# The last 128-row output tile of a fused attention and MoE kernel, computed as two 256-column halves in two PSUM banks

## The chip, the cores and the metric

One core of a Trainium2 chip runs the kernel. The metric is the device time of one execution in microseconds (us). Before the change the median of 4 runs is 301.82 us (301.5 to 302.29). One further quantity is used throughout: the profiled execution, whose own time is 301.5 us and whose span, from its first to its last recorded instruction, is 299.7 us. About 0.2% (0.6 us) is what a measurement of this kernel can tell from no change.

## The reference

The reference computes a linear attention (softmax of q over the head dimension, softmax of k over the sequence, k-transposed times v, then q times that) and feeds the result as rows into a two-layer network with an ELU between. Only the last step is touched by the change, the second matrix product:

```python
h = x @ w_in                      # x: 4608 x 512, w_in: 512 x 2048
g = np.where(h > 0.0, h, np.exp(np.minimum(h, 0.0)) - 1.0)
return (g @ w_out)                # w_out: 2048 x 512, result 4608 x 512, float32
```

## The kernel before

The 4608 rows are worked in 9 blocks of 512. For each block, eight groups `g` compute 256 rows of the transposed hidden layer (line 543, 16 matmuls of 512 columns into a two-bank PSUM tile), ScalarE (ACT) takes the exponential (line 559), VectorE (DVE) finishes the ELU and writes the group into the tile `GT` in SBUF (lines 576 and 578). The second product follows one block behind: a 128-row output tile `ts` of a block `jb` is a sum over 16 slices `jj` of `GT`, so 16 matmuls, each with its own 128x128 weights (a slice of `GT`) and 512 moving columns (a slice of `W2`), all in fp32r, into one PSUM bank (`out_mm`, line 582, matmul on line 588). Every matmul instruction is a weight load (shown as PEld) and a matmul (shown as PE).

`out_store` (line 595) then has ACT copy the bank to one of three SBUF tiles `OSB` (line 605) and sends two stores of 64 rows of 2,048 bytes (128 KB each) to DRAM (line 615). All stores go through SP's queue, but the second one of the very last tile is issued from ACT's (line 614), so that the last two stores are issued at once.

After the last block's groups, nothing is left but output tiles: the last half of the block before's last tile, and then the four tiles `ts` = 0 to 3 of the last block (lines 797 to 802), alternating between PSUM banks 4 and 5. The first of them is split in 14 and 2 matmuls, as the last group of `GT` arrives late.

What runs on which engine in which order is not left to a scheduler: `ORDER` holds a table of operation numbers for each engine, written out by hand. Numbers are given in the order in which `add` is called. `Sched.order` walks the tables with an estimate of every duration only to merge the engines into one program; within an engine the table's order holds. `Sched.emit` (line 178) puts a semaphore wait before an operation for each dependency on another engine or a DMA. At the end SP waits for all store semaphores whose names begin with "o" (lines 223 to 225), in the order in which they were made; there are 15.

Of the kernel before, what the change touches and what calls it, by code (L numbers as in the profile page):

```python
# [3 lines left out]
AF = mybir.ActivationFunctionType  # L4
# [7 lines left out]
B, H, S, D = 8, 8, 576, 64  # L12
DFF = 2048
BLK = 512
NBLK = B * S // BLK
RING = 3 * BLK
NU = 2 * B
CH = 9
# [3 lines left out]
ISSUE = {"sp": 550, "act": 550, "gp": 740}  # L22
# [7 lines left out]
        "518 461 496 469 501 526 509 564 514 572 522 538 585 527 540 568 577 573 598 581 586 590 594 "  # L30
        "603 611 549 607 636 599 556 657 640 612 662 644 649 653 645 670 622 666 624 683 688 658 679 "
        "632 675 671 634 696 709 684 692 701 714 697 705 722 727 735 718 710 740 731 748 723 744 761 "
        "736 766 757 753 749 770 787 762 774 779 775 783 788 792 793 797 801 805 "),
    "act": (
        "3 22 33 23 24 31 29 34 35 48 44 55 73 76 77 79 83 84 87 94 95 97 104 91 92 116 117 119 98 "
        "108 120 127 135 133 163 160 179 147 166 154 169 205 176 230 231 188 234 180 240 241 191 246 "
# [3 lines left out]
        "493 467 484 531 489 453 460 463 506 519 462 497 470 502 542 510 515 565 537 523 539 554 551 "  # L40
        "528 569 578 574 541 552 616 582 591 587 595 548 555 550 608 637 600 626 557 604 641 613 650 "
        "654 621 646 623 663 667 689 631 625 659 680 633 676 672 685 693 715 702 698 635 706 719 728 "
        "711 732 741 724 745 737 767 758 750 771 754 763 776 780 784 789 794 798 802 806 808 "),
    "dve": (
        "2 4 5 0 6 7 25 26 37 27 38 39 40 41 42 36 46 49 51 52 53 56 74 75 78 80 81 85 88 89 96 100 "
        "105 106 101 102 122 118 110 111 112 123 124 141 142 143 148 155 182 183 184 177 178 232 206 "
# [14 lines left out]
        "229 228 323 315 288 295 316 289 324 298 341 359 308 360 377 307 340 393 370 371 406 394 420 "  # L61
        "380 407 419 447 433 390 465 482 432 458 448 389 494 481 495 459 468 478 507 520 535 477 567 "
        "508 521 536 553 566 546 580 547 579 620 605 638 606 593 592 630 651 652 639 677 665 690 664 "
        "678 703 716 717 691 730 704 729 756 768 769 742 755 743 782 791 781 790 800 795 799 796 803 "
        "804 807 "),
}


# [159 lines left out]
def t_act(n, psum):  # L228
    return n / 1.2 + (70 if psum else 99)


def t_dve(n, fast=1):
    return n / 0.96 / fast + 74


def t_f32r(n):
    return (n + 32) / 2.4


class Gen:  # L240
# [338 lines left out]
                gt, esb[:, :], P[:, :], ALU.max), key,  # L579
                R=[f"E{i}"], W=gw, X=banks)  # L580

    def out_mm(self, jb, ts, bk, jj0, jj1, key):
        S = self.S
        GT, dst = self.GT[jb % 2], self.bank(bk)

        def mm(e):
            for jj in range(jj0, jj1):
                last = e.matmul(dst, GT[:, jj, ts * 128:(ts + 1) * 128], self.W2[:, jj, :],  # L588
                                start=(jj == 0), stop=(jj == 15))
            return last  # L590
        S.add("pe", (jj1 - jj0) * t_f32r(512), mm, key, side=2,
              R=[f"G{jb % 2}_{g}" for g in range(jj0 // 2, (jj1 + 1) // 2)] +
                [f"W2_{s}" for s in range(jj0 // 4, (jj1 + 3) // 4)], X=[f"b{bk}"])

    def out_store(self, jb, ts, bk, key, eng="act"):
        S = self.S
        if jb == 0:
            i, osb = f"x{ts}", self.OSB0[ts]
        else:
            i = self.oslot % len(self.OSB)  # L600
            self.oslot += 1
            osb = self.OSB[i]
        src = self.bank(bk)
        if eng == "act":
            S.add("act", t_act(512, True), lambda e: e.activation(osb[:, :], src, AF.Copy), key,  # L605
                  W=[f"O{i}0", f"O{i}1"], X=[f"b{bk}"])
        else:
            S.add("dve", t_dve(512), lambda e: e.tensor_copy(osb[:, :], src), key,
                  W=[f"O{i}0", f"O{i}1"], X=[f"b{bk}"])
        rows = self.out.rearrange("(b p c) f -> b c p f", p=64, c=CH)  # L610
        for x in range(2):
            gi = 8 * jb + 2 * ts + x
            b, c = gi // CH, gi % CH
            q = "act" if x and gi == 8 * NBLK - 1 else "sp"
            S.add(q, ISSUE[q], lambda e, b=b, c=c, x=x: e.dma_start(
                rows[b, c], osb[x * 64:(x + 1) * 64, :]), key, R=[f"O{i}{x}"],
                dma=f"o{i}{x}{q}", nbytes=64 * 2048)
            S.ops[-1].packet, S.ops[-1].margin = 2048, 300

    def program(self):  # L620
        S = self.S
# [123 lines left out]
        key = 0  # L745
# [48 lines left out]
        assert not work  # L794
        self.out_mm(*w, key)
        self.out_store(w[0], w[1], w[2], key + 1)
        for ts in range(4):
            bk = 4 + ts % 2
            for jj0, jj1 in ((0, 14), (14, 16)) if ts == 0 else ((0, 16),):
                self.out_mm(NBLK - 1, ts, bk, jj0, jj1, key)  # L800
            self.out_store(NBLK - 1, ts, bk, key)
            key += 1


# [33 lines left out]
```

The softmax here doesn't subtract the row's maximum and nothing guards it: scores larger than these inputs give would overflow.

## Time and profile before

| What | Value |
|---|---|
| median of 4 runs | 301.82 us |
| profiled execution, its time | 301.5 us |
| profiled execution, its span | 299.7 us |
| what lies around the span (time less span) | 1.8 us |
| PE (TensorE matmul) busy | 287.0 us, 96% of the span |
| PEld (weight load) busy | 235.4 us, 79% |
| DVE busy | 189.5 us, 63% |
| ACT busy | 182.3 us, 61% |
| granted TensorE clock, mean | 0.998 |
| one 128x512 copy of a PSUM bank by ACT (line 605) | 597 ns |
| start of the last tile's first matmul | 292.23 us |
| start of the last tile's copy by ACT | 296.06 us |
| issue of the last two stores | 296.68 us |

An engine's share of the span says how busy it was; with PE at 96% the kernel is one long row of matmuls. A matmul's own duration in the profile (389 ns for 512 columns) is longer than the distance between the starts of two of them (227 ns), since they are pipelined: for the cost of a matmul the starts are to be read. "Time to landing" of a store runs from its issue until its semaphore is complete. Times within the execution are counted from the span's start.

### The profile page before, as it was taken

To read this page: it belongs to the slowest core of one execution; us is meant where nothing else is said; L and a number is where in the kernel's file an instruction comes from. 1 tells how busy PE (TensorE), PEld (TensorE's weight loads), DVE (VectorE), ACT (ScalarE), POOL (GpSimd) and SP (SyncE) were. 2 spreads that over 40 slices of the span, in tenths; PEclk is the share of its full clock that TensorE was granted. 3 is DMA by queue.
4 is the path that set the end of the run, shared out by engine and by line. 5 is a ranking of instruction groups with operands and counts; after the bars stand their busy time and mean duration, and the time that the engine had idled before them with its cause. 6 is when DMAs were issued, how large, how long until landed. Compare 5 with 4: busy or idle time off the path is not lost.

```text
span 299.7 us, 4412 instructions
## 1 busy us (share of the span) xinstructions
PE 287.0 (96%) x1849; PEld 235.4 (79%) x1849; DVE 189.5 (63%) x244; ACT 182.3 (61%) x211; POOL 21.7 (7%) x33
## 2 busy tenths in 40 slices
PE   1699999999999999999999999999999999999995
PEld 1578877677888888888888888888888888888883
DVE  3948934985898685894568855588437256655400
ACT  5758848998977967867755767534562423432411
POOL 0960234100000000000000000000000000000000
PEclk9999999999999999999999999999999999999999
DMA  7999998995497895289436236041311302004223
GB/s 263 388 399 391 388 391 257 235 328 198 118 277 229 125 363 172 76 258 276 163 116 167 87 90 159 2 104 40 78 44 44 72 0 53 0 0 107 56 60 94
DMA packets 35283, 49.96 MB, mean 167 GB/s; under 512 B 16320, under 2 KB 16320, under 8 KB 35264
## 3 DMA queue, kind: packets, MB, share of 16 engines
q1 hardware_dynamic: 29680, 34.09, 41.1%
q0 software_dynamic: 5504, 15.47, 16.1%
q8 instruction: 14, 0.23, 0.3%
q10 hardware_dynamic: 80, 0.13, 0.1%
q14 instruction: 5, 0.04, 0.0%
HBM read 36.70 MB, written 9.44 MB: 154 GB/s over the span
## 4 chain that ended last, share of the span: by engine, by line
PE 94%; DVE 2%; ACT 2%; DMA 1%; issue 0%
PE PS L588 44%; PE PS L543 43%; PE PS L487 3%; PE PS L456 2%; DMA QR<-in_q_dram 1%; PE PS L403 1%; DVE ZQ L372 1%; ACT ESB L559 1%; DVE QS L380 0%; DVE GT L572 0%; ACT QR L352 0%; PE PS L653 0%; ACT ESB L570 0%; ACT OSB L605 0%; DVE RZQ L376 0%
## 5 line engine op out<-in xcount | busy, mean ns | idle before, releaser
L588 PE MATMUL PS<-W,GT 128*128 128x512 f32 x576 | 141.2, 392 | 0.4 <-DVE GT L578 0.4
L543 PE MATMUL PS<-XT,W 128*128 128x512 f32 x576 | 140.4, 391 | 0.1
L543 PEld LDWEIGHTS PS<-XT,W 128*128 128x128 f32 x576 | 107.2, 188 | 23.0 <-DVE GT L572 0.5
L588 PEld LDWEIGHTS PS<-W,GT 128*128 128x128 f32 x576 | 106.8, 188 | 22.6 <-DVE GT L578 0.8
L559 ACT ACTIVATE ESB<-PS 128x1024 f32<-128x1024 f32 x72 | 73.7, 1027 | 64.9 <-PE PS L543 64.7
L576 DVE TENSOR_SCALAR ESB<-ESB 128x1024 f32<-128x1024 f32 x64 | 44.1, 691 | 66.6 <-ACT ESB L559 65.9
L578 DVE TENSOR_TENSOR GT<-ESB,PS 128x1024 fp32r<-128x1024 f32 x64 | 77.7, 1217 | 1.8
L605 ACT ACTIVATE OSB<-PS 128x512 f32<-128x512 f32 x32 | 18.8, 597 | 32.2 <-PE PS L588 32.0
L372 DVE TENSOR_REDUCE ZQ<-QR 128x18 f32<-128x1152 f32 x16 | 21.5, 1343 | 7.2 <-ACT QR L352 7.2
L509 ACT ACTIVATE XT<-PS 128x512 fp32r<-128x512 f32 (+6 forms) x32 | 19.5, 608 | 8.6 <-PE PS L487 8.1
L380 DVE TENSOR_TENSOR QS<-QR,RZQ 128x1152 f16<-128x1152 f32 x16 | 21.6, 1353 | 0.3
L352 ACT ACTIVATE QR<-QR 128x1152 f32<-128x1152 f32 x16 | 18.6, 1165 | 2.8 <-DMA QR<-in_q_dram 2.8
L356 ACT ACTIVATE KR<-KR 128x1152 bf16<-128x1152 f32 x16 | 18.5, 1160 | 1.7 <-DMA KR<-in_k_dram 1.7
L487 PE MATMUL PS<-qsT,MBLK 128*128 128x320 f32 (+5 forms) x64 | 14.4, 312 | 0.0
L431 ACT ACTIVATE qsT<-QT 128x1152 fp32r<-128x1152 f16 x12 | 14.0, 1165 | 0.3 <-DMA QT<-QS 0.3
L487 PEld LDWEIGHTS PS<-qsT,MBLK 128*128 128x128 f32 x64 | 11.9, 194 | 2.7 <-DVE MBLK L469 0.5
L365 ACT ACTIVATE VB<-VR 128x1152 bf16<-128x1152 f32 (+1 forms) x12 | 13.5, 1125 | 0.6 <-DMA VR<-in_v_dram 0.6
L572 DVE SCALAR_TENSOR_TENSOR GT<-PS,ESB 128x1024 fp32r<-128x1024 f32 x8 | 9.8, 1221 | 4.5 <-ACT ESB L570 4.4
L403 PE MATMUL PS<-ID,QS 128*128 128x128 f16 x36 | 3.7, 266 | 6.7 <-DVE QS L380 6.7
L469 DVE TENSOR_TENSOR MBLK<-PS,RZK 64x128 fp32r<-64x128 f32 x32 | 9.2, 288 | 0.9
L403 PEld LDWEIGHTS PS<-ID,QS 128*128 128x128 f16 x36 | 2.9, 122 | 7.3 <-DVE QS L380 7.0
L570 ACT ACTIVATE ESB<-ESB 128x1024 f32<-128x1024 f32 x8 | 8.5, 1060 | 0.2
(28 smaller groups left out, 60.0 us busy)
## 6 DMA issues: line engine op xcount, KB each, us to landing
out_dram<-OSB SPq DMA_DIRECT2D x63, 128.0 KB, 2.4
QR<-in_q_dram SPq DMA_DIRECT2D x12, 576.0 KB, 5.0
KR<-in_k_dram SPq DMA_DIRECT2D x12, 576.0 KB, 5.6
VR<-in_v_dram SPq DMA_DIRECT2D x12, 576.0 KB, 5.4
W<-in_moe_w_out_dram POOLq DMA_DIRECT2D x4, 1024.0 KB, 18.9
QR<-in_q_dram POOLq DMA_DIRECT2D x4, 576.0 KB, 11.4
KR<-in_k_dram POOLq DMA_DIRECT2D x4, 576.0 KB, 11.5
VR<-in_v_dram POOLq DMA_DIRECT2D x4, 576.0 KB, 8.1
```

The lines of the kernel that those rows point to most:

```text
L352: S.add("act", t_act(1152, False), lambda e: e.activation(flat(q), flat(q), AF.Exp), key - 3, X=[f"qR{i}"], follow=self.table)
L356: S.add("act", t_act(1152, False), lambda e: e.activation(ek[:, :, :, :].rearrange("p h c d -> p (h c d)"), flat(k), AF.Exp), key - 2, X=[ ...
L372: S.add("dve", t_dve(1152), lambda e: e.tensor_reduce(self.ZQ[i][:, :, :].rearrange("p h c -> p (h c)"), q[:, :, :, :].rearrange("p h c d ...
L380: S.add("dve", t_dve(1152), lambda e: e.tensor_tensor(qso, q[:, :, :, :], rz, ALU.mult), key - 3, R=[f"qR{i}", f"RZQ{i}"], W=[f"QS{self.al ...
L487: last = e.matmul(P[:, y:y + n_], M[:, f, :], T[:, c0:c1, f * 64:f * 64 + 64], start=True, stop=True)
L509: S.add("act", t_act((h1 - h0) * n_, True), lambda e, dst=dst, src=src: e.activation(dst, src, AF.Copy), key, W=W, X=X)
L543: last = e.matmul(P[:, t * 512:(t + 1) * 512], self.W1[:, kc, tt * 128:(tt + 1) * 128], self.XT[:, kc, rc:rc + BLK], start=(kc == 0), stop ...
L559: S.add("act", t_act(1024, True), lambda e: e.activation(esb[:, :], P[:, :], AF.Exp), key, W=[f"E{i}"], X=banks)
L576: S.add("dve", t_dve(1024, 2), lambda e: e.tensor_scalar(esb[:, :], esb[:, :], 1.0, -1.0, ALU.min, ALU.add), key, X=[f"E{i}"])
L578: S.add("dve", t_dve(1024), lambda e: e.tensor_tensor(gt, esb[:, :], P[:, :], ALU.max), key, R=[f"E{i}"], W=gw, X=banks)
L588: last = e.matmul(dst, GT[:, jj, ts * 128:(ts + 1) * 128], self.W2[:, jj, :], start=(jj == 0), stop=(jj == 15))
L605: S.add("act", t_act(512, True), lambda e: e.activation(osb[:, :], src, AF.Copy), key, W=[f"O{i}0", f"O{i}1"], X=[f"b{bk}"])
```

## The change

The four tiles of the last block become three full ones and two halves of the fourth. Each half has 16 matmuls of 256 columns: columns 0 to 255 go to PSUM bank 0, and columns 256 to 511 go to bank 5. In PE's table the first half (operation 805) stands right behind the first full tile, ahead of the other two (797, 801); the second half (809) stands last. In ACT's table the first half's copy (806) stands behind the copy of the second full tile (798). Each half is copied on its own (128x256) into its half of the same `OSB` tile and stored with two stores of 64 rows of 1,024 bytes; the second half's second store goes through ACT's queue. In SP's table the stores are also put in the order of their tiles. The halves' four stores have semaphores of their own, so that SP waits for 18 at the end. DVE's and GpSimd's instructions stay as they are. The diff, with the tables cut to the rows that differ:

```diff
# "pe"
-        "736 766 757 753 749 770 787 762 774 779 775 783 788 792 793 797 801 805 "),
+        "736 766 757 753 749 770 787 762 774 779 775 783 788 792 793 805 797 801 809 "),
# "act"
-        "711 732 741 724 745 737 767 758 750 771 754 763 776 780 784 789 794 798 802 806 808 "),
+        "711 732 741 724 745 737 767 758 750 771 754 763 776 780 784 789 794 798 806 802 810 812 "),
# "sp"
-        "678 703 716 717 691 730 704 729 756 768 769 742 755 743 782 791 781 790 800 795 799 796 803 "
-        "804 807 "),
+        "678 703 716 717 691 730 704 729 756 768 769 742 755 743 782 781 790 791 795 796 799 800 807 "
+        "808 803 804 811 "),
...
-    def out_mm(self, jb, ts, bk, jj0, jj1, key):
+    def out_mm(self, jb, ts, bk, jj0, jj1, key, c0=0, c1=512):
         S = self.S
-        GT, dst = self.GT[jb % 2], self.bank(bk)
+        GT, dst = self.GT[jb % 2], self.bank(bk)[:, c0:c1]
 
         def mm(e):
             for jj in range(jj0, jj1):
-                last = e.matmul(dst, GT[:, jj, ts * 128:(ts + 1) * 128], self.W2[:, jj, :],
+                last = e.matmul(dst, GT[:, jj, ts * 128:(ts + 1) * 128], self.W2[:, jj, c0:c1],
                                 start=(jj == 0), stop=(jj == 15))
             return last
-        S.add("pe", (jj1 - jj0) * t_f32r(512), mm, key, side=2,
+        S.add("pe", (jj1 - jj0) * t_f32r(c1 - c0), mm, key, side=2,
...
+    def last_store(self, bk, osb, i, c0, c1, key):
+        S, n_ = self.S, c1 - c0
+        src = self.bank(bk)[:, c0:c1]
+        S.add("act", t_act(n_, True), lambda e: e.activation(osb[:, c0:c1], src, AF.Copy), key,
+              W=[f"O{i}{x}{c0}" for x in range(2)], X=[f"b{bk}"])
+        rows = self.out.rearrange("(b p c) f -> b c p f", p=64, c=CH)
+        for x in range(2):
+            gi = 8 * NBLK - 2 + x
+            b, c = gi // CH, gi % CH
+            q = "act" if x and c0 else "sp"
+            S.add(q, ISSUE[q], lambda e, b=b, c=c, x=x: e.dma_start(
+                rows[b, c][:, c0:c1], osb[x * 64:(x + 1) * 64, c0:c1]), key, R=[f"O{i}{x}{c0}"],
+                dma=f"o{i}{x}{c0}{q}", nbytes=64 * 1024)
+            S.ops[-1].packet, S.ops[-1].margin = 1024, 300
...
-            q = "act" if x and gi == 8 * NBLK - 1 else "sp"
+            q = "sp"
...
-        for ts in range(4):
+        for ts in range(3):
             bk = 4 + ts % 2
             for jj0, jj1 in ((0, 14), (14, 16)) if ts == 0 else ((0, 16),):
                 self.out_mm(NBLK - 1, ts, bk, jj0, jj1, key)
             self.out_store(NBLK - 1, ts, bk, key)
+            key += 1
+        i = self.oslot % len(self.OSB)
+        for bk, c0 in ((0, 0), (5, 256)):
+            for x in range(2):
+                name = f"O{i}{x}"
+                S.w[name + str(c0)] = S.w.get(name, [])
+                S.r[name + str(c0)] = list(S.r.get(name, []))
+            self.out_mm(NBLK - 1, 3, bk, 0, 16, key, c0, c0 + 256)
+            self.last_store(bk, self.OSB[i], i, c0, c0 + 256, key)
             key += 1
```

## The prediction

> **What bounds the kernel now.** First the page's chain of work that ended last and its busy times: PE has 94% of the chain and is busy 96% of the span, at full clock in every slice. So outside the start and the end, a microsecond is won or lost only on PE. Next the same chain in order of time, its last rows (start, length, engine, tile, line):
>
> ```profile
> 276.07 3.63 PE PS L543 x16
> 279.70 16.33 PE PS L588 x72
> 296.03 0.02 issue
> 296.06 0.60 ACT OSB L605
> ```
>
> The reader is to see that from 279.70 PE runs 72 output matmuls without a gap: 16.33 / 72 = 0.2268 us each, 3.63 us for a tile. Only behind the last of them do other engines set the end. The timeline of the end (start, length, what; in brackets the idle time before) has the rest:
>
> ```profile
> 294.73 1.29 PE L588 MATMUL PS<-W,GT 128*128 128x512 f32 x5
> ...
> 296.06 0.60 ACT L605 ACTIVATE OSB<-PS 128x512 f32<-128x512 f32 x1 [3.03 <-PE PS L588]
> 296.68 0.47 SPq L615 DMA_DIRECT2D out_dram<-OSB  x1
> 296.68 0.55 ACTq L615 DMA_DIRECT2D out_dram<-OSB  x1
> ```
>
> The last matmul starts at 295.63; 0.425 later ACT starts its copy (296.06), the stores are issued at 296.68 and land 2.32 (SP's) and 2.60 us (ACT's) later, at 299.29. SP's last waits and the barrier take until 299.67. The DMA view of this end shows when bytes move, in slices of 0.0925 us from 296:
>
> ```profile
> DMA  0000000000000000000679899789984000000000
> ...
> out_dram<-OSB SPq DMA_DIRECT2D x1, 128.0 KB, 2.3
> out_dram<-OSB ACTq DMA_DIRECT2D x1, 128.0 KB, 2.6
> ```
>
> Of ACT's 2.60 us, about 1.12 pass before the first packet (297.80), 1.14 are packets (to 298.94), 0.35 the way to the semaphore. In the packet records SP's packets of 2,048 bytes took 145 ns, then more as ACT's joined; ACT's go out behind them at 84 ns each, four per DMA engine.
>
> **The change part by part.** All sums are against the profiled execution (span 299.7, time 301.5, which is 0.32 under the median of 301.82); the difference is then put on the median.
>
> *The two halves on PE.* Removed are 16 matmuls of 512 columns: 16 x 0.2266 = 3.63 us. Added are 32 of 256, each with its own weight load. The nearest rows are 256-column fp32r matmuls of line 487, in pairs, each with a weight load, between 512-column ones:
>
> ```profile
> 44.29 0.40 PE L487 MATMUL PS<-qsT,MBLK 128*128 128x256 f32 x2
> 44.53 0.40 PE L588 MATMUL PS<-W,GT 128*128 128x512 f32 x1
> ```
>
> Two take 44.53 - 44.29 = 0.24; in the ten such pairs of the trace the starts lie 118 to 120 ns apart, and the next matmul 118 to 122 behind, except where a bf16 row follows. So 32 x 0.120 = 3.84, and **+0.21 us**. Is a run of 16 as fast as a pair? A weight load must fit into each 120 ns. The row for that are four 64-column matmuls with four weights:
>
> ```profile
> 30.76 0.53 PE L487 MATMUL PS<-qsT,MBLK 128*128 128x64 f32 x4
> 31.12 0.47 PE L588 MATMUL PS<-W,GT 128*128 128x512 f32 x1
> ```
>
> Their starts settle at 110 to 112 ns: the pace of weight loads alone. It fits under 120. The low bound is thus 32 x 0.112 = 3.58 (-0.04). The high bound is the recorded length of a weight load, 188 ns, if nothing overlapped: 6.02 (+2.39). I take 120 because pace and partner are the same there.
>
> The Trainium skill weighs in here ("TensorE: Matmul & The Clock Gate", section "Back-to-back issue gap"): an isolated warm gap of N/2.4 + 2.5 ns, 109 for 256 columns and 216 for 512, by which the split would cost 32 x 0.109 - 16 x 0.216 = +0.04. This trace has 120 and 227, some 11 ns more for each matmul, and the measurement decides.
>
> *The first half, run ahead.* Its 16 matmuls start where the second full tile did (284.98) and need nothing late: bank 0 was last read by DVE for group 6, done by 280.94, and the last group of `GT` was already needed by the two matmuls before. Its copy (128x256) stands behind that of the second full tile, now 288.80 + 1.92 = 290.72 to 291.32, and goes until about 291.8; the next copy is due at 294.35. ACT idles 3.03 us before each of these copies, so this is hidden; without that cover it would cost its 0.39. Its `OSB` tile must be free of the first full tile's stores: with SP's new order these are issued near 285.8 and 286.3 and land by 288.7, ahead of 291.3. SP's two further issues (0.47 to 0.60 each) lie between 292.5 and 293.7; those of the third full tile follow at 294.97 and 295.48 and are through at 296.08, before the last ones at 296.7. If SP were late, the last store would be by as much; 0.6 us of slack is there. The waits of PE on ACT (banks 4 and 5) keep at least one full tile between.
>
> *The second half, at the end.* It starts at 292.23 + 1.92 = 294.15; its last matmul at 294.15 + 15 x 0.120 = 295.95. The copy follows a 256-column matmul by 0.32 (44.41 to ACT's 44.73), so at 296.27: 0.21 later than before. The copy:
>
> ```profile
> L605 ACT ACTIVATE OSB<-PS 128x512 f32<-128x512 f32 x32 | 18.8, 597 | 32.2 <-PE PS L588 32.0 <-DMA out_dram<-OSB 0.2
> ...
> L509 ACT ACTIVATE XT<-PS 128x256 fp32r<-128x256 f32 x1 | 0.4, 392 | 0.0
> ```
>
> 597 - 392 = 0.205 is saved (line 509 has 597 for 512 columns too, so the type costs nothing). The copy ends at 296.66, as before: **PE's loss and the copy's gain cancel, +0.01**.
>
> *The last two stores*, 64 KB in place of 128 KB, with as many packets (64 data and 16 semaphore). No row has a 1,024-byte store, so bounds. If packets are paced by their number, nothing is gained: 0. If all time scales with bytes, half of the 1.14 us: 0.57. Rows between: packets of 256, 2,048 and 2,304 bytes took 18, 84 and 93 ns at their fastest, a line of about 9 ns + 0.0366 ns per byte, so 46 for 1,024. ACT's four packets behind SP's then save 4 x (84 - 46) = 0.15. SP's four at 145 would go to some 77, and save 0.27, if they wait for bytes, and almost nothing if for descriptors. For bytes speaks that they follow each other on an engine without gaps. I take bytes: **-0.42**, with 0 and -0.57 as ends.
>
> A rule against this gain stands in the skill's "DMA: Bandwidth & Descriptors", section "Measured (HBM→SBUF, 128 partitions, SWDGE, issued from GpSimd)": 64 packets take at least about 0.67 us however small, and transfers under 64 KB are descriptor-dominated. An isolated store here has its 64 packets within 0.67 to 0.75 us (118 us into the span). By that rule SP's store gains nothing and the term would be -0.15.
>
> *SP's final waits.* Before, the built program waits for eight pairs of semaphores; the trace has them resume at 299.01 with SP's store and step every 60 ns until the barrier at 299.46, 0.17 behind ACT's landing. After, nine pairs end with ACT's and SP's last halves; from ACT's landing two steps remain, 0.02 + 2 x 0.065 = 0.15. **-0.02**, between 0 and -0.1.
>
> **Sum**: +0.01 - 0.42 - 0.02 = -0.43. Span 299.27, profiled time 301.07; on the median 301.82 - 0.43 = **301.4 us**, 0.14% faster, within the 0.2% (0.6 us) that a measurement can tell from no change.
>
> **Rivals.**
> 1. *The stores are paced by packets, not bytes.* For it: an isolated store moves only some 190 GB/s where long loads reach over 400. Against it: no gaps between its packets. The store term is 0 to -0.19; 301.8 to 301.6.
> 2. *All packet time scales with bytes*, both queues together: -0.57 + 0.01 - 0.1 (the end of SP's waits too), 301.16; just over 0.2% faster.
> 3. *Slower: the weight loads set the pace of a long run of 256 columns.* Place: both halves on PE, all on the path. It decides from a pace of 120 + 430/32 = 133 ns on, where the gain of 0.43 is used up, and makes it slower by 0.6 us at 152 ns. At 188 ns it costs 2.39 in place of 0.21: 301.4 + 2.2 = 303.6. Against it: the load pace of 110 to 112 ns.
> 4. *It doesn't do what it says*: the last half's stores stay behind those of the third full tile, issued 1.2 us before. Price: up to one store's 0.64 us spacing, 301.39 + 0.64 = 302.0. Against it: a row of stores 0.64 us apart lands each after 2.36 us, as a lone one does after 2.23.
>
> **How the numbers follow.** Forecast 0.50, rival 1 0.22, rival 2 0.15, rival 3 0.06, rival 4 0.07. Faster by over 0.2% (below 301.2): rival 2 and a part of the forecast by the runs' own spread of 0.8 us, 0.22. Slower (above 302.4): rival 3 and a little of 4, 0.07. The rest, 0.71, is within. The range reaches from rival 2, widened on the fast side to 301.0 by a part of that spread, to rival 4 with 302.0, rounded up to 302.1. Rival 3 is left out.
>
> **What would show it.** Starts 120 ns apart in both halves (152 or more: rival 3); the last copy starting near 296.27 and taking 0.39; ACT's last store landing 2.2 us after issue (2.4 or more: rival 1; 2.05 or less: rival 2); no idle PE between 285 and 296. Wrong would be above all a store time that does not answer to bytes.

## The result, and the profile after

The changed kernel takes 301.16 us (median of 42 runs, 300.34 to 302.1), the kernel before, run beside it, 301.51 (67 runs, 300.68 to 303.36). The ratio is 0.9985, 95% interval 0.9977 to 0.9992: 0.24 to 0.69 us faster, some 0.45. The two means lie 0.47 apart, the two medians 0.35. The forecast was -0.43. Its 301.4 us counted from the median of 4 runs, 301.82, which is 0.31 above the one of 67.

The chain of waits that ended last, after (start, length, engine, tile, line; the same rows as shown of before):

```profile
275.99 3.63 PE PS L543 x16
279.62 16.56 PE PS L588 x88
296.17 0.02 issue
296.20 0.38 ACT OSB L598
```

PE's last stretch has 88 matmuls in 16.56 us in place of 72 in 16.33: 0.23 more for the split. The copy behind it takes 0.38 in place of 0.60.

The timeline of the end, after:

```profile
290.66 0.60 ACT L620 ACTIVATE OSB<-PS 128x512 f32<-128x512 f32 x1 [4.97 <-PE PS L588]
291.15 0.38 ACT L598 ACTIVATE OSB<-PS 128x256 f32<-128x256 f32 x1
292.44 1.24 SPq L605 DMA_DIRECT2D out_dram<-OSB  x2
294.29 0.60 ACT L620 ACTIVATE OSB<-PS 128x512 f32<-128x512 f32 x1 [2.75 <-PE PS L588]
294.91 1.11 SPq L630 DMA_DIRECT2D out_dram<-OSB  x2
296.20 0.38 ACT L598 ACTIVATE OSB<-PS 128x256 f32<-128x256 f32 x1 [1.31 <-PE PS L588]
296.61 0.47 SPq L605 DMA_DIRECT2D out_dram<-OSB  x1
296.61 0.54 ACTq L605 DMA_DIRECT2D out_dram<-OSB  x1
```

The reader is to see that the first half's copy (291.15) and its two stores (292.44) lie where ACT and SP would idle, and that SP is through with the third full tile's stores at 296.02, 0.6 ahead of the last issue. The DMA view of the end, in slices of 0.0925 us from 296 (the first hump is the third full tile's stores, the second one the last half's); below it the last stores, with KB each and us to landing:

```profile
DMA  6799992869979210002698896300000000000000
...
out_dram<-OSB SPq DMA_DIRECT2D x1, 128.0 KB, 2.4
out_dram<-OSB SPq DMA_DIRECT2D x1, 64.0 KB, 1.9
out_dram<-OSB ACTq DMA_DIRECT2D x1, 64.0 KB, 2.2
```

Packets of the last stores now fill 8 of these slices where they filled 12, and the two stores land 1.9 and 2.2 us after issue in place of 2.3 and 2.6.

The spans cannot be compared as they stand. The start of the last line-543 matmul, ahead of which the code of all kernels in this study is the same, lies between 278.95 and 280.65 us in the twelve profiles, the first line-543 matmul already between 14.92 and 15.68. So all profiles below are compared from the start of that last line-543 matmul to the span's end, which I call the **stretch**. It is 20.363 us before, 19.950 after and 19.953 in a second profile of the changed kernel. Its parts, in us:

| Part of the stretch | before | after | difference | forecast |
|---|---|---|---|---|
| last line-543 matmul to last matmul | 16.320 | 16.653 | +0.333 | +0.32 |
| last matmul's start to the copy's | 0.425 | 0.316 | -0.109 | -0.105 |
| the copy | 0.597 | 0.383 | -0.214 | -0.205 |
| the copy's end to the issue of the stores | 0.026 | 0.026 | 0 | 0 |
| issue to landing (SP's issue to ACT's landing, the later one) | 2.608 | 2.214 | -0.394 | -0.42 |
| landing to SP's barrier | 0.173 | 0.143 | -0.030 | -0.02 |
| barrier to the span's end | 0.214 | 0.215 | 0 | 0 |
| sum | 20.363 | 19.950 | -0.413 | -0.43 |

### The profile page after: what moved, and what is told of

It reads as the page before. It is cut to its first block, busy times and chain, and to the rows that moved or that the text cites. A ratio compares the mean times of both kernels' runs of the same rounds, so it can differ in the third digit from the quotient of the medians.

```text
span 299.2 us, 4448 instructions
## 1 busy us (share of the span) xinstructions
PE 287.0 (96%) x1865; PEld 236.0 (79%) x1865; DVE 189.6 (63%) x244; ACT 182.3 (61%) x212; POOL 21.7 (7%) x33
## 4 chain that ended last, share of the span: by engine, by line
PE 94%; DVE 2%; ACT 2%; DMA 1%; issue 0%
PE PS L588 44%; PE PS L543 43%; PE PS L487 3%; PE PS L456 2%; DMA QR<-in_q_dram 1%; PE PS L403 1%; DVE ZQ L372 1%; ACT ESB L559 1%; DVE QS L380 0%; DVE GT L572 0%; ACT QR L352 0%; ACT ESB L570 0%; PE PS L668 0%; ACT OSB L598 0%; DVE RZQ L376 0%
## 5 line engine op out<-in xcount | busy, mean ns | idle before, releaser
L588 PE MATMUL PS<-W,GT 128*128 128x512 f32 (+1 forms) x592 | 141.6, 386 | 0.4 <-DVE GT L578 0.4
L620 ACT ACTIVATE OSB<-PS 128x512 f32<-128x512 f32 x31 | 18.2, 598 | 31.5 <-PE PS L588 30.8
```

## The experiments

My theory: the smaller last stores are the whole gain, PE's loss and the shorter copy cancel, and running ahead hides only hidden work. Against it stand rival 1 (stores paced by the number of packets), rival 3 (weight loads), rival 4 (nearby stores), and a fifth: the gain comes from SP's straightened order and its waits. The first four runs take the change apart. In the diffs `...` stands for lines left out: rearranged tables of operation numbers and the passing of arguments.

**Half stores alone.** On the kernel before (columns 0 to 255 of the last 128 rows are never stored):

```diff
+            s0 = 256 if gi >= 8 * NBLK - 2 else 0
...
-                rows[b, c], osb[x * 64:(x + 1) * 64, :]), key, R=[f"O{i}{x}"],
+                rows[b, c][:, s0:], osb[x * 64:(x + 1) * 64, s0:]), key, R=[f"O{i}{x}"],
```

> The kernel before, with one edit: the last tile's two stores carry columns 256 to 511 alone (64 rows of 1,024 bytes each); the other half of the last 128 rows is never stored. Theory (store time follows bytes, and that is the whole gain): the last store lands 2.2 us after its issue in place of 2.60, the execution is 0.4 us shorter, ratio 0.9987, 301.1 if before is at 301.5. Rival 1 (stores are paced by the number of packets): 2.45 to 2.6 us, 0 to 0.15 us shorter. Rival 5 (the gain comes from SP's straightened order and its waits): 2.6 us, nothing.

Measured: ratio 0.9988 (0.9971 to 1.0004); the last store lands 2.196 us after issue; the stretch is 20.002, 0.361 shorter. Landing alone gives 0.40; SP's waits, still in their old order, give 0.04 back. The time's interval includes 1 and is too wide by itself, but the landing is the theory's, and neither rival's. The rows of the DMA view for its last two stores (KB each, us to landing):

```profile
out_dram<-OSB SPq DMA_DIRECT2D x1, 64.0 KB, 2.0
out_dram<-OSB ACTq DMA_DIRECT2D x1, 64.0 KB, 2.2
```

**Half copy alone.** On the kernel before (the last tile's first half of columns is an older tile's):

```diff
-            S.add("act", t_act(512, True), lambda e: e.activation(osb[:, :], src, AF.Copy), key,
+            s0 = 256 if (jb, ts) == (NBLK - 1, 3) else 0
+            S.add("act", t_act(512, True), lambda e: e.activation(
+                osb[:, s0:], src[:, s0:], AF.Copy), key,
```

> The kernel before, with one edit: the last tile's copy by ACT takes columns 256 to 511 alone; the stores carry whole rows, whose first halves are an older tile's. Theory: the copy takes 0.38 us in place of 0.60 and the stores are issued as much earlier, 0.21 us shorter, ratio 0.9993. A rival in which the copy is not on the path: nothing, with the same distance from the last matmul to the stores' issue (1.05 us) as before.

Measured: ratio 0.9992 (0.9977 to 1.0007); the copy takes 0.384, the stores land after 2.604 as before, the stretch is 20.143: 0.220 shorter. The stretch is as the theory expected; the time's interval includes 1. The copy's row:

```profile
295.69 0.38 ACT L606 ACTIVATE OSB<-PS 128x256 f32<-128x256 f32 x1 [3.03 <-PE PS L588]
```

**Split matmuls alone.** On the kernel before, the halves go to banks 0 (its second 256 columns) and 1 (its first), side by side, so that one copy takes both:

```diff
...
-        for ts in range(4):
+        for ts in range(3):
...
+        for bk, c0, at in ((0, 0, 256), (1, 256, 0)):
+            self.out_mm(NBLK - 1, 3, bk, 0, 16, key, c0, c0 + 256, at)
+        self.out_store(NBLK - 1, 3, 0, key, src=self.PS[0][:, 256:768], banks=["b0", "b1"])
```

> The kernel before, with the split on PE alone: the last tile's matmuls are two halves of 16 matmuls of 256 columns in two PSUM banks, the first half run ahead as in the change, but then one copy of 512 columns and two stores of 128 KB as before. Theory: 32 matmuls at 120 ns in place of 16 at 227, 0.21 us longer, ratio 1.0007, the store term unchanged (2.60 us). Rival 3 (a long run of 256 columns is set by weight loads): starts 130 to 188 ns apart, 0.5 to 2.4 us longer.

Measured: ratio 1.0008 (0.9993 to 1.0023), stretch 20.589, 0.226 longer; the starts within the halves lie 120 ns apart in the median. Rival 3 is out for 256 columns by these starts; the time's interval includes 1. Its chain, to be read beside the two above: PE's 88 matmuls as after, the copy as before.

```profile
279.38 16.56 PE PS L588 x88
295.93 0.02 issue
295.96 0.60 ACT OSB L605
```

The three parts alone add up to -0.361 - 0.220 + 0.226 = -0.355; the changed kernel has -0.413. The 0.06 between lie in SP's waits: with small stores the old order is 0.212 behind the landing, the new one 0.143.

**Whole last stores in the changed kernel.** The reverse of the first run:

```diff
...
+        if not c0:
+            return
...
-                rows[b, c][:, c0:c1], osb[x * 64:(x + 1) * 64, c0:c1]), key, R=[f"O{i}{x}{c0}"],
+                rows[b, c], osb[x * 64:(x + 1) * 64, :]), key, R=[f"O{i}{x}0", f"O{i}{x}256"],
...
```

> The changed kernel, with one edit: the first half gets no stores of its own, and the last two stores carry whole rows of 2,048 bytes, as before the change. Matmuls, copies and SP's new order stay. Theory (the store's size is the whole gain): the last store lands 2.6 us after issue again, and the gain is gone, ratio to before 1.000 (0.9995 to 1.0005), 0.4 us above the changed kernel. Rival 5 (order and waits): as fast as the changed kernel, 0.9985.

Measured: the last store lands after 2.618, the stretch is 20.360, within 3 ns of before: SP's new order, the split and the half copies together are worth nothing without the small stores. The last two stores:

```profile
out_dram<-OSB SPq DMA_DIRECT2D x1, 128.0 KB, 2.3
out_dram<-OSB ACTq DMA_DIRECT2D x1, 128.0 KB, 2.6
```

The timing does not say this: the ratio is 0.9987 (0.9974 to 1.0000), where 1.000 was expected and 0.9985 was the rival's. Its upper end only touches 1.000. The medians are 0.06 us apart (301.44 and, before, 301.50). Twelve runs, with a start that varies by more than the effect, do not tell the two apart; the trace's stretch does, and I go by it.

The next three runs change the changed kernel, and a fourth repeats it.

**Narrow last stores.** In the changed kernel the second half's stores carry 64 columns (columns 256 to 447 of the last tile are never stored):

```diff
+            s0 = 448 if c0 else 0
...
-                rows[b, c][:, c0:c1], osb[x * 64:(x + 1) * 64, c0:c1]), key, R=[f"O{i}{x}{c0}"],
+                rows[b, c][:, s0:c1], osb[x * 64:(x + 1) * 64, s0:c1]), key, R=[f"O{i}{x}{c0}"],
```

> The changed kernel, with one edit: the second half's two stores carry its last 64 columns alone (64 rows of 256 bytes, 16 KB each); columns 256 to 447 of the last tile are never stored. Theory (bytes): packets of some 18 to 25 ns in place of 46 to 80, the packets' phase shrinks from 0.74 to 0.25 to 0.35 us, the last store lands 1.7 to 1.8 us after issue, 0.4 to 0.5 us under the changed kernel, ratio to before 0.997. Rival 1 (a floor by the number of packets): the phase stays at 0.6 to 0.7 us, the landing at 2.1 to 2.2, ratio 0.998 to 0.9985.

Measured: ratio 0.9985 (0.9971 to 0.9998), stretch 19.733, 0.22 under the changed kernel; landing after 1.993. That is neither: bytes go on paying, but half as much as the theory had it. The DMA view from the last issue (slices of 0.0593 us; the hump on the left is the third full tile's stores) shows why:

```profile
DMA  2949969679131000000353014420000000000000
...
out_dram<-OSB SPq DMA_DIRECT2D x1, 16.0 KB, 1.7
out_dram<-OSB ACTq DMA_DIRECT2D x1, 16.0 KB, 2.0
```

There are two small humps with a hole between. SP's 64 packets (18 ns each) begin 1.12 us after issue and are out at 1.34, 0.22 us for all 64, so their number sets no floor of 0.6 us: rival 1 falls. ACT's begin at 1.40, when SP's are already out.

**First half not run ahead.**

```diff
-... 792 793 805 797 801 809
+... 792 793 797 801 805 809
-... 794 798 806 802 810 812
+... 794 798 802 806 810 812
-... 795 796 799 800 807 808 803 804 811
+... 795 796 799 800 803 804 807 808 811
```

> The changed kernel, with the first half not run ahead: it stands directly before the second half on PE, its copy behind the third full tile's on ACT, its stores behind that tile's on SP. Theory (running ahead hides only work that is hidden anyway): as fast as the changed kernel within 0.1 us, ratio to before 0.9985; SP is through with the first half's stores near 295.9, ahead of the last issue at 296.6. Rival 4 (nearby stores hold up the last ones): the last stores land up to 0.6 us later, ratio up to 1.0005.

Measured: ratio 0.9984 (0.9972 to 0.9997), stretch 19.946, 4 ns from the changed kernel's. The timeline of its end: the first half's copy, its stores, and the last copy and issue.

```profile
294.96 0.38 ACT L598 ACTIVATE OSB<-PS 128x256 f32<-128x256 f32 x1 [1.31 <-PE PS L588]
295.37 2.38 SPq L605 DMA_DIRECT2D out_dram<-OSB  x3
296.88 0.38 ACT L598 ACTIVATE OSB<-PS 128x256 f32<-128x256 f32 x1 [1.53 <-PE PS L588]
297.29 0.55 ACTq L605 DMA_DIRECT2D out_dram<-OSB  x1
```

Even 1.92 us before the last copy, the first half's copy and its two issues fit. Running ahead is worth nothing here. Rival 4 is out by SP's last store: with stores of 2,048-byte rows it lands 2.318 us after issue in the kernel before, where the nearest store was issued 3.12 us ahead of it, and 2.317 in the run with whole last stores, where that was 1.19.

**Quarters.** In the changed kernel the second half becomes two times 128 columns:

```diff
...
-        for bk, c0 in ((0, 0), (5, 256)):
+        for bk, c0, c1 in ((0, 0, 256), (1, 256, 384), (5, 384, 512)):
...
```

> The changed kernel, with the second half cut in two quarters of 128 columns in banks 1 and 5, the first of them behind the second full tile; the last copy takes 128 columns and the last stores 512-byte rows. Theory (weight loads need 112 ns each): 32 matmuls at 112 ns in place of 16 at 120, 1.66 us more on PE, less 0.1 for the copy and 0.2 to 0.3 for the stores: 1.3 us longer than the changed kernel, ratio to before 1.003. Rival (the matmul's time follows its columns, some 67 ns for 128): 0.2 us more on PE, so 0.1 us shorter than the changed kernel, ratio 0.998.

Measured: ratio 1.0040 (1.0026 to 1.0054), stretch 21.358, 1.41 over the changed kernel. Its chain:

```profile
279.55 18.23 PE PS L588 x104
297.78 0.02 issue
297.81 0.28 ACT OSB L598
```

Starts of the 128-column matmuls lie 111 ns apart (median), though 128 columns are half of 256: the pace of the prediction's 64-column row, each matmul there too with a weight load. Only the first matmul of each run of 16, which stands behind 512 columns, is followed after 57 ns, so a 128-column matmul by itself does not need 111. The weight loads themselves start 108 to 112 ns apart, which speaks for them as what sets the pace; no run has these matmuls without their loads. 18.23 - 16.56 = 1.67 us more on PE (1.66 expected) against 0.11 for the copy and 0.17 for the store. The pace that rival 3 feared exists; at 256 columns it does not bind yet, at 128 it does.

**The changed kernel again.**

> The changed kernel once more, for the comparison on this chip. Ratio 0.9985, the last store landing 2.21 us after its issue.

Measured: ratio 0.9983 (0.9970 to 0.9996), stretch 19.953, landing after 2.213.

Two further variants of the changed kernel, each executed once and profiled, are about the hole between SP's and ACT's packets. One execution says nothing of the time, so only their traces are read.

**ACT's store alone** (64 rows' second half is never stored):

```diff
...
         for x in range(2):
+            if c0 and not x:
+                continue
```

> The changed kernel, with the second half's store on SP's queue left out (columns 256 to 511 of 64 of the last 128 rows are never stored); ACT's stays. With small stores ACT's first packet never came earlier than 1.39 to 1.41 us after its issue, where SP's comes at 1.12. If ACT's packets wait for SP's (their making or their sending), ACT alone starts at 1.12 and lands at about 1.93. If ACT's queue is slower by itself, it starts at 1.40 again and lands at 2.2.

Measured: the first packet comes 1.20 us after issue, the landing at 2.022. Neither end: alone, ACT's first packet is 0.08 later than SP's (1.20 against 1.12), and 0.20 more is added when SP issues at the same time. The 0.08 goes with the issuing instruction, which takes 551 ns on ACT and 467 on SP: from its end to the first packet pass 0.65 us here and 0.66 on SP. What the 0.20 is, the making of the descriptors or their sending, stays open. The store's row in the DMA view:

```profile
out_dram<-OSB ACTq DMA_DIRECT2D x1, 64.0 KB, 2.0
```

**Both on SP's queue:**

```diff
...
-            q = "act" if x and c0 else "sp"
+            q = "sp"
```

> The changed kernel, with both of the second half's stores on SP's queue. SP issues the second 0.51 us behind the first. The store then lands about 0.51 + 2.05 = 2.56 us after the first one's issue, in place of 2.21: 0.35 us longer from the last matmul to the end, if the issue is what spaces them; as long as before (2.2) if the packets of the first are what the second waits for anyway.

Measured: the second issue is 0.509 behind the first, and it lands 2.562 after the first one's issue (2.56 expected); the stretch is 20.243, 0.29 over the changed kernel: 0.35 later landing, less 0.06 that SP's waits behind it are shorter. In the DMA view of its end (from 297, slices of 0.0875 us) the last two stores stand apart, as their issues do:

```profile
DMA  4696959299997931000048961003887200000000
```

So ACT's queue, though later, is right for the second store.

## Why the prediction was right, point by point

The sum, -0.43 against -0.413 in the stretch and some -0.45 in the times, came out closer than the times can show (0.24 to 0.69 faster); what supports the prediction are its terms, each read from the stretch. That 301.16 lies below the forecast 301.4 is mostly the kernel before itself, which beside it took 301.51 and not 301.82.

*The bound.* PE ran its last stretch without a gap in every profile, and only what stands behind the last matmul and the length of the matmuls themselves moved the end.

*The two halves on PE.* 120 ns from a pair of another line held for runs of 16 (median 120 in every profile that has them). The term came out at +0.22 to the start of the copy (+0.333 - 0.109), against +0.21. The low bound's row, the pace of weight loads, turned out to be the pace one step further (111 ns at 128 columns); its high bound, a weight load's recorded length, is none: with one load for each matmul, starts 111 to 120 ns apart show that a load does not take these 188 ns of PE's time.

The Trainium skill's rule that was weighed here, the isolated gap of N/2.4 + 2.5 ns in "TensorE: Matmul & The Clock Gate", section "Back-to-back issue gap", is below what was measured in these runs of matmuls: 120 ns at 256 columns against its 109.

*The first half, run ahead.* Rightly costed at nothing, and shown to earn nothing either: without it the stretch is 4 ns shorter.

*The copy.* -0.214 against -0.205; alone it gave 0.220.

*The last two stores.* -0.394 against -0.42: right in sign and total, less right in its parts, and the closeness of the total is partly luck. The forecast was 0.27 from SP's packets, behind which ACT's would follow, and 0.15 from ACT's own. In the packet records ACT's first packet came 0.34 earlier (1.743 us after its issue before, 1.406 after), and ACT's own packets saved only 0.07 (0.52 us from the first to the last before, 0.45 after): they take some 69 ns each in the median, where the forecast had 46 from the line through the fastest. Two misses of 0.07 and 0.08 nearly cancel.

By the time from SP's first packet to ACT's last the sizes line up as 1.14 us (2,048 bytes a packet), 0.74 (1,024), 0.59 (512) and 0.50 (256): the first halving saves 0.40, the next ones 0.15 and 0.09, about 0.37 us for every 1,024 bytes on top of 0.40 that do not shrink. I had taken ACT's packets to start when SP's are through. At 2,048 bytes their first one, at 1.74, comes with the first of SP's 16 semaphore packets (1.74 to 1.94), and at 1,024, at 1.41, just behind it (1.39). But at 512 bytes ACT's begin at 1.39, and at 256 at 1.40 with SP's gone at 1.34: a smaller store of SP's does not bring them earlier. So 0.28 of the 0.40 that remain are ACT's later start; by their number alone 64 packets of SP need no more than 0.22. The upper end of the store term (-0.57, all packet time in proportion to bytes) was out of reach for the same reason.

The skill's rule against this gain, a floor of 0.67 us for 64 packets ("DMA: Bandwidth & Descriptors", section "Measured (HBM→SBUF, 128 partitions, SWDGE, issued from GpSimd)"), did not hold for these stores, which are not the loads issued from GpSimd that the page measured: SP's 64 packets of 256 bytes went out in 0.22 us.

*SP's final waits.* -0.030 against -0.02. The old order holds at SP's last store and then takes 0.45 us for the waits that follow; before, 0.29 of that passed while ACT's store was still to land, so that only 0.17 was left behind it. With half-sized stores ACT's landing comes 0.25 after SP's, and the old order would have cost 0.07 (0.212 against 0.143).

*The rivals.* Packets by number and weight loads at 256 columns are out, each by a run of its own, and nearby stores by SP's unchanged landing; the fifth, SP's order, by the whole last stores' stretch (not by their time) and by the half stores, which have the gain in the old order. All of this is read from traces, one of each kernel and two of the changed one.

## What to carry to other kernels

At the end of this kernel, the work behind the last matmul (copy, store, waits) is a path of its own, and cutting the last piece in two shortened it by part of what that piece copied and stored; the copy paid for the split and the smaller store was the gain. Cut no finer than the pace of the matmuls allows: from 256 to 128 columns PE lost 1.67 us and copy and store won back 0.3. When the effect is 0.1% and the start of the kernel varies by more, compare profiles from a common instruction near the end: parts that the timing could not separate repeated there within 30 ns from kernel to kernel.

## What the runs showed of the hardware that was not expected

- A store issued from ACT's queue had its first packet 1.20 us after issue when alone. When SP issued at the same time, it had it at 1.39 to 1.41 with packets of 1,024 bytes or less, at 1.73 to 1.74 with 2,048. SP's store of the last two, or the first of the two where both were on its queue, had it at 1.12 in every run.
- A longer issuing instruction moved a store's first packet by as much. With both last stores on SP's queue the second took 597 ns to issue, the first 467, and their first packets came 1.25 and 1.12 us after issue; from the end of the instruction that is 0.65 to 0.66 us, as for ACT's store alone.
- Ahead of the end, the same instructions took between 278.95 and 280.65 us in the twelve profiles. Of these 1.7 us, at most 0.76 was there by the first line-543 matmul; where the rest arises was not looked into.
